# Upper weight words limited by one ScalarE step for all 16 tiles, and a new order of all engines, in a gated linear attention plus MoE kernel

## Chip, cores and metric

One core of a Trainium2 chip. The metric is the device time of one execution in microseconds (us), lower is better; before the change the median of three runs is 465.81 us (465.54 to 467.68).

## What is computed

```python
f = 1 / (1 + exp(-f_logit))                       # [4, 8, 768, 48]
state = 0                                         # [4, 8, 48, 48]
for t in range(768):
    state = f[:, :, t, :, None] * state + k[:, :, t] (outer) v[:, :, t]
    y[:, :, t] = q[:, :, t] @ state
x = y as [3072 tokens, 384]
h = x @ w_in                                      # 384 -> 2048
g = h * clip(h + 3, 0, 6) / 6
out = g @ w_out                                   # 2048 -> 384
```

All arrays are float32; the weights reach the kernel as float64 words (`w`, viewed as int64) and are turned on the chip into two fp32r parts, a high and a low one.

## The kernel before

The attention is cut into 24 units (4 batches times 6 chunks of 128 tokens). The MoE is cut into 6 groups of 512 tokens (the four units of one chunk) times 16 weight tiles `f`; step `n` of the MoE stands for group `n // 16` and tile `n % 16`. Everything is written out as one list of tokens, `ORDER`, from which the program emits the instructions; `after` chains each engine's instructions, so each engine runs its own instructions in exactly that order. `ON_POOL` names the tokens that GpSimd does in place of VectorE, `ON_ACT` those weight tiles whose limiting is done on ScalarE. A token is an operation and a number; a TensorE token also has the PSUM bank it writes.

Tokens of a unit, with the line of the kernel before: on SyncE's queue `load` L352 (gates), `loadq` L359 (q and k), `loadv` L364 and `hole` L568 (two copies into the gaps of the transposed activations `xts`); on ScalarE `gate` L369, `end` L395, `ktok` L470, `xh` L550, and `carry0`, `carry1` L495, L502 of units 0 to 3; on VectorE `back` L376, `rend` L392, `fwd` L400, `kmul` L389, `qmul` L405, `decay` L408 (the last three may be on GpSimd), `mask` L451, `xl` L563, `carry0`, `carry1` L497, L504 of the later units; on TensorE `tk` L463, `kv` L482, `att` L444, `qs` L514, `av` L531. In some units `xl` is done by TensorE and ScalarE (`ym` L554, `xl` L561).

Tokens of weight tile `f`: `ld` L256 (768 KB from HBM into `raw`), `z` L279 on ScalarE (rounds the word, into `w`), the limit of the upper 16 bits into `y`, `mid` L286, `dif` L291 and `top` L295 on VectorE (they put the exponent in place), `high` L307 on ScalarE, `low` L310 on VectorE (or in two parts `lowi`, `lowo`), `wd` L314 (a copy that keeps fp32 output weights). The limit is the subject: for the nine tiles of `ON_ACT` it is two ScalarE steps, `cy` L267 (relu of the word plus a bias, reading `raw` with a stride) and `lim` L271 (relu of a constant less that, in place); for the other seven it is one VectorE `lim` L273.

Tokens of a MoE step: `mm1` L599 (9 matmuls of 512 columns), `relu` L609 on ScalarE, `g` L613 on VectorE, `gh` L622 on ScalarE, `gl` L626 on VectorE or GpSimd, `mm2` L643 (9 matmuls). Tiles 0 to 2 of the first group are done in halves of 256 columns: `mm1a`, `mm1b` L665 (units 0 and 1, units 2 and 3), `relua` L674, `ga` L679, `mm2a`, `mm2b` L684. `warm` L822 and `tiny` L829 are matmuls on a blank tile with which TensorE fills time. Buffers are rings: `qkf` 3, `v` 3, `gates` 2, `tg` 3, `gg` 2, `w` 3, `y` 2.

Of the kernel before, what the change touches and what calls it, by code (L numbers as in the profile page):

```python
# [59 lines left out]
warm.2 carry0.1 mask.1 high.0 wd.0 qs.1.0 back.3 av.1 loadq.4 hole.0 att.2.2 xh.1 dif.1 kmul.3 warm.4 z.1 xl.1 load.4  # L60
mask.2 ktok.2 hole.1 lowi.0 cy.2 rend.3 top.1 tk.3.4 warm.2 ld.3 kv.2.2 ktok.3 lim.2 kv.3.0 fwd.3 carry0.2 z.2 warm.2
mid.2 qs.2.2 qmul.3 warm.2 carry1.3 dif.2 load.5 att.3.0 gate.4 ld.4 top.2 av.2 high.1 wd.1 mm1a.0.4 loadv.4 carry0.3
mask.3 lowi.1 end.3 carry1.2 loadq.5 xh.2 back.4 warm.1 high.2 ym.2 qs.3.0 relua.0 av.3 lowi.2 xl.2 kmul.4 lim.3
warm.1 xh.3 hole.2 mm1a.1.2 ga.0 end.4 xl.3 mm2a.0 relua.1 hole.3 decay.4 gate.5 ga.1 mid.3 z.3 rend.4 mm1a.2.1 dif.3
ld.5 fwd.4 wd.2 cy.4 ld.6 tk.4.4 mm2a.1 loadq.6 lim.4 qmul.4 top.3 ktok.4 ld.7 z.4 att.4.2 load.6 mid.4 ld.8 mm1b.0.4
back.5 relua.2 ld.9 high.3 ld.14 mm1b.1.0 ga.2 kmul.5 relub.0 rend.5 gb.0 cy.5 dif.4 kv.4.2 ld.10 mm1b.2.1 low.3 lim.5
loadv.5 top.4 mm2b.0 z.5 carry0.4 relub.1 mid.5 mm2a.2 mask.4 high.4 gb.1 cy.6 carry1.4 dif.5 mm2b.1 low.4 relub.2
lim.6 top.5 tk.5.0 mm1.3.3 z.6 mid.6 fwd.5 mm1.4.4 dif.6 qmul.5 relu.3 gb.2 end.5 high.5 g.3 decay.5 gate.6 low.5
att.5.2 ktok.5 mm2b.2 relu.4 back.6 top.6 qs.4.0 kmul.6 av.4 loadq.7 g.4 high.6 loadv.6 mask.5 loadv.7 mm1.5.4 gh.3
ld.12 lim.7 gh.4 load.7 low.6 ld.11 xh.4 gl.4 ld.15 gl.3 mm2.3 relu.5 rend.6 z.7 g.5 mid.7 z.8 lim.8 mm2.4 dif.7 gh.5  # L70
top.7 z.9 mid.8 mm1.6.2 high.7 dif.8 cy.9 low.7 end.6 top.8 kv.5.0 decay.6 relu.6 tk.6.4 lim.9 mm1.7.3 carry0.5 xl.4
gl.5 cy.10 mid.9 high.8 fwd.6 qs.5.0 relu.7 av.5 dif.9 qmul.6 mm2.5 xh.5 loadv.8 carry1.5 g.7 loadq.8 ktok.6 g.6 z.10
low.8 ym.5 lim.10 mm1.8.4 top.9 gate.7 gh.6 back.7 high.9 att.6.2 mid.10 gh.7 kv.6.0 kmul.7 gl.6 mm2.6 cy.11 rend.7
mask.6 lim.11 dif.10 z.11 low.9 tk.7.2 mm1.9.3 top.10 ktok.7 relu.8 fwd.7 high.10 end.7 relu.9 low.10 gl.7 mm2.7 g.8
carry0.6 gh.8 mm1.10.4 g.9 cy.12 carry1.6 qmul.7 xl.5 mid.11 load.9 gl.8 lim.12 mm2.8 ld.13 decay.7 hole.5 dif.11 gh.9
mid.12 z.12 dif.12 qs.6.2 top.11 att.7.0 loadq.9 top.12 av.6 high.11 load.8 kv.7.0 relu.10 gl.9 mm2.9 low.11 xh.6
carry0.7 mask.7 z.14 g.10 gate.9 qs.7.0 xl.6 z.13 lim.13 av.7 hole.6 mid.13 mm1.11.2 xh.7 lim.14 gh.10 loadv.9 dif.13
hole.4 mid.14 high.12 gl.10 mm2.10 top.13 relu.11 gate.8 g.11 low.12 gh.11 mm1.12.3 high.13 gl.11 carry1.7 xl.7 low.13
hole.7 mm1.13.4 dif.14 loadq.10 top.14 mm2.11 back.8 high.14 relu.12 low.14 kmul.8 z.15 mm1.14.1 lim.15 relu.13 g.12
g.13 mid.15 mm1.16.0 gh.13 dif.15 top.15 gl.13 tk.8.2 high.15 mm2.13 end.8 gh.12 low.15 relu.14 rend.8 gl.12 mm1.15.4  # L80
fwd.8 qmul.8 mm2.12 back.9 relu.15 load.10 relu.16 g.15 ktok.8 g.14 att.8.2 g.16 kv.8.2 gh.14 mm1.17.4 mask.8 gl.14
rend.9 gate.10 fwd.9 gh.15 mm2.14 gl.15 qmul.9 back.10 mm2.15 lowo.0 mm1.19.1 outs.0 outv.1 kmul.9 end.9 gh.16 outs.2
gl.16 decay.8 relu.17 mm1.18.0 od.2 rend.10 load.11 relu.19 g.17 od.0 carry0.8 fwd.10 mm2.16 relu.18 g.19 end.10
qmul.10 carry1.8 g.18 tk.9.3 kmul.10 load.12 lowo.1 mm1.20.4 loadv.10 ktok.9 od.1 gh.17 decay.9 gh.18 gl.17 gate.11
qs.8.0 back.11 att.9.2 decay.10 loadq.11 av.8 kv.9.2 gl.18 xh.8 mm2.17 gate.12 carry0.9 carry1.9 lowo.2 end.11 mask.9
mm1.21.2 gh.19 gl.19 xl.8 tk.10.3 relu.21 mm2.18 ktok.10 g.21 relu.20 rend.11 back.12 qs.9.0 gh.21 fwd.11 att.10.2
loadq.12 av.9 kv.10.0 qmul.11 mm2.19 g.20 load.13 loadv.11 carry0.10 gl.21 loadv.12 carry1.10 mm1.22.4 rend.12 fwd.12
kmul.12 mask.10 mm2.21 relu.22 g.22 decay.11 gh.22 kmul.11 mm1.23.3 gate.13 qmul.12 xh.9 back.13 load.14 hole.8
tk.11.4 relu.23 gl.22 mm2.22 ktok.11 xl.9 gh.20 g.23 hole.9 gl.20 qs.10.0 rend.13 att.11.2 gate.14 loadq.13 av.10
kv.11.0 loadv.13 tk.12.4 mm2.20 ktok.12 gh.23 end.12 gl.23 decay.12 mm1.24.4 mask.11 kmul.13 mm1.25.3 mm2.23 relu.25  # L90
relu.24 g.25 g.24 mm1.29.3 gh.24 gl.24 fwd.13 mm1.26.4 relu.29 gh.25 qmul.13 xh.10 gl.25 mm2.25 load.15 xl.10 relu.26
carry0.11 back.14 mm2.24 g.29 g.26 qs.11.0 gh.26 att.12.2 gl.26 av.11 kv.12.2 loadv.14 xh.11 carry1.11 mm2.26 mask.12
hole.10 gh.29 carry0.12 gate.15 carry1.12 loadq.14 rend.14 mm1.27.4 tk.13.2 relu.27 mm1.30.3 g.27 gl.29 xl.11 mm2.29
relu.30 hole.11 gh.27 g.30 end.13 kmul.14 mm1.28.1 gl.27 gh.30 ktok.13 gl.30 decay.13 back.15 tk.14.0 mm2.30 fwd.14
qmul.14 mm1.31.2 load.16 mm1.32.4 relu.31 relu.28 g.31 end.14 g.28 mm2.27 relu.32 ktok.14 qs.12.0 gh.28 att.13.2 gh.31
loadq.15 gl.28 av.12 kv.13.2 g.32 xh.12 mm2.28 decay.14 gate.16 mask.13 rend.15 carry0.13 carry1.13 fwd.15 mm1.33.4
xl.12 qmul.15 gl.31 qs.13.2 kmul.15 att.14.0 load.17 loadv.15 av.13 kv.14.0 xh.13 mm2.31 relu.33 xl.13 back.16 hole.13
tk.15.2 g.33 mm1.35.3 end.16 loadq.16 ktok.15 hole.12 carry0.14 gh.32 end.15 outs.3 outv.4 gl.32 decay.15 loadv.16
gate.17 mm1.36.2 rend.16 fwd.16 gh.33 outs.5 relu.35 mm2.32 g.35 qmul.16 carry1.14 gl.33 load.18 mm1.34.4 gh.35
kmul.16 back.17 mm2.33 relu.34 relu.36 g.34 g.36 tk.16.3 gl.35 gh.34 mm1.41.4 ktok.16 gl.34 mask.14 qs.14.2 att.15.0  # L100
loadq.17 decay.16 av.14 od.5 kv.15.0 xh.14 mm2.35 xl.14 mask.15 carry0.15 rend.17 mm2.34 fwd.17 gh.36 relu.41 qmul.17
g.41 qs.15.0 gl.36 gh.41 att.16.2 av.15 gl.41 kv.16.2 xh.15 mm2.36 gate.18 back.18 mm2.41 carry0.16 rend.18 xl.15
fwd.18 hole.15 mm1.38.4 carry1.16 loadv.17 mask.16 load.19 carry1.15 loadv.18 loadq.18 mm1.40.0 relu.38 mm1.37.3
relu.40 mm1.39.1 relu.37 g.37 qmul.18 g.38 mm1.44.3 kmul.17 gh.38 load.20 hole.14 g.40 gl.38 mm1.43.0 relu.39 gh.40
gl.40 mm2.38 g.39 relu.43 mm2.40 gh.37 end.18 gate.20 gl.37 g.43 mm1.42.1 kmul.18 gh.39 end.17 relu.44 gl.39 g.44
mm2.39 mm2.37 mm1.47.2 gh.44 gh.43 relu.42 gl.43 mm1.46.0 g.42 relu.47 gl.44 g.47 mm2.44 mm2.43 gh.42 gl.42 mm1.51.3
gh.47 relu.46 gl.47 back.20 mm1.45.2 g.46 tk.18.0 relu.45 mm2.42 ktok.18 g.45 relu.51 g.51 tk.17.4 gh.46 mm2.47
ktok.17 gl.46 gate.19 qs.16.0 gh.45 att.17.2 loadq.19 decay.18 gl.45 av.16 kv.17.0 mask.17 mm2.46 xh.16 decay.17
mm1.49.3 mm2.45 relu.49 g.49 carry0.17 xl.16 mm1.48.4 outs.6 back.19 outs.8 gh.51 od.8 od.3 qs.17.0 relu.48 att.18.2
# [857 lines left out]
```

## Time and profile before

| | |
|---|---|
| median of three runs | 465.81 us (465.54, 465.81, 467.68) |
| span of the profiled execution | 464.7 us (its own time is not listed apart) |
| TensorE busy | 453.4 us, 98% of the span |
| VectorE, ScalarE, GpSimd busy | 291.0, 212.4, 64.3 us |
| mean granted TensorE clock | 0.998 |
| chain that ended last | TensorE 90%, VectorE 3%, DMA 2%, ScalarE 2% |

Busy time of TensorE is an upper bound of its use, since matmuls are pipelined and their ends are modelled. The page divides the span in 40 slices of 11.6 us: VectorE is near full in the first 10 of them and at about half afterwards, ScalarE is busiest in the second to eighth, and the DMA engines are near full in the first five.

### The profile page before, as it was taken

How to read it: one execution, taken by the hardware profiler on the slowest of the kernel's cores; microseconds unless marked ns; L12 is line 12 of the kernel's file. 1: busy time of each engine (PE TensorE's matmuls, PEld its weight loads, DVE VectorE, ACT ScalarE, POOL GpSimd, SP SyncE). 2: the span in 40 equal slices, each digit the busy share in tenths (PEclk: the TensorE clock that was granted, in tenths of full speed). 3: DMA queues.
4: the chain of work that ended last, by engine and by line, in shares of the span. 5: the costliest groups of instructions: out<-in, count | busy, mean ns of one | idle time of the engine just before them, and what ended most of it. 6: DMA issues, size and time to landing. Idle time of an engine off the chain costs nothing.

```text
span 464.7 us, 11482 instructions
## 1 busy us (share of the span) xinstructions
PE 453.4 (98%) x4967; PEld 386.6 (83%) x4967; DVE 291.0 (63%) x455; ACT 212.4 (46%) x365; POOL 64.3 (14%) x65
## 2 busy tenths in 40 slices
...
GB/s 302 306 294 335 360 242 24 204 54 26 176 108 104 24 81 59 132 74 84 82 0 1 110 75 155 56 57 2 95 1 20 8 1 0 2 135 1 0 1 74
DMA packets 19113, 44.91 MB, mean 97 GB/s; under 512 B 2544, under 2 KB 8816, under 8 KB 19056
## 3 DMA queue, kind: packets, MB, share of 16 engines
...
q14 instruction: 16, 0.13, 0.1%
...
## 4 chain that ended last, share of the span: by engine, by line
PE 90%; DVE 3%; DMA 2%; ACT 2%; issue 1%; SPq 0%; POOL 0%; POOLq 0%
PE o L643 35%; PE pair L599 26%; PE single L599 11%; PE pair L514 3%; PE pair L444 2%; DMA v<-unit 2%; PE pair L531 2%; PE o L684 2%; PE idle L822 2%; PE pair L482 2%; PE pair L699 1%; PE single L699 1%; PE pair L463 1%; PE pair L665 1%; ACT w L279 1%
## 5 line engine op out<-in xcount | busy, mean ns | idle before, releaser
L643 PE MATMUL o<-gg,weight 128*128 128x512 f32 x705 | 165.7, 382 | 0.4 <-DVE gg L626 0.3
L643 PEld LDWEIGHTS o<-gg,weight 128*128 128x128 f32 x705 | 131.1, 189 | 19.8 <-DVE gg L626 1.6
L599 PE MATMUL pair<-xts,weight 128*128 128x512 f32 x576 | 133.1, 381 | 0.0
L599 PEld LDWEIGHTS pair<-xts,weight 128*128 128x128 f32 x576 | 107.6, 189 | 15.1 <-DVE tg L613 0.3
L626 DVE TENSOR_TENSOR gg<-tg,gg 128x512 fp32r<-128x512 f32 x75 | 56.0, 751 | 55.6 <-ACT gg L622 55.4
L622 ACT ACTIVATE gg<-tg 128x512 fp32r<-128x512 f32 x79 | 48.9, 626 | 65.7 <-PE o L643 51.3
L613 DVE SCALAR_TENSOR_TENSOR tg<-tg,pair 128x512 f32<-128x512 f32 x64 | 43.4, 683 | 55.8 <-ACT tg L609 55.6
L609 ACT ACTIVATE tg<-pair,half 128x512 f32<-128x512 f32 x64 | 43.5, 684 | 72.4 <-PE pair L599 69.1
L599 PE MATMUL single<-xts,weight 128*128 128x512 f32 x261 | 61.9, 382 | 0.0
L599 PEld LDWEIGHTS single<-xts,weight 128*128 128x128 f32 x261 | 48.5, 189 | 7.0 <-DVE tg L613 0.2
L609 ACT ACTIVATE tg<-single,half 128x512 f32<-128x512 f32 x29 | 19.9, 685 | 32.8 <-PE single L599 29.2
L376 DVE TENSOR_TENSOR_SCAN suffix<-gates,unit 112x516 f32<-112x516 f32 (+1 forms) x25 | 29.4, 1180 | 4.2 <-ACT gates L369 4.2
L400 DVE TENSOR_TENSOR_SCAN gates<-gates,rend 112x516 f32<-112x516 f32 x24 | 30.4, 1266 | 0.3
L389 POOL TENSOR_TENSOR qkf<-qkf,suffix 112x512 f32<-112x512 f32 x14 | 21.1, 1507 | 64.7 <-DVE suffix L376 22.2
L613 DVE SCALAR_TENSOR_TENSOR tg<-tg,single 128x512 f32<-128x512 f32 x29 | 19.8, 682 | 9.9 <-ACT tg L609 9.6
L408 POOL TENSOR_TENSOR decayed<-state,ends 112x192 f32<-112x192 f32 x13 | 10.6, 819 | 109.8 <-PE pair L514 65.8
L405 POOL TENSOR_TENSOR qkf<-qkf,gates 112x512 f32<-112x512 f32 x11 | 15.8, 1437 | 67.0 <-DVE gates L400 39.3
L550 ACT ACTIVATE xts<-pair 112x512 fp32r<-112x512 f32 x24 | 14.2, 594 | 23.6 <-PE pair L531 19.0
L451 DVE TENSOR_TENSOR a<-pair,causal 128x512 f32<-128x512 f32 x24 | 16.4, 683 | 8.2 <-PE pair L482 5.3
L643 PE MATMUL o<-xts,weight 128*128 128x512 f32 x84 | 20.3, 380 | 0.0
L563 DVE TENSOR_TENSOR xts<-pair,xts 112x512 fp32r<-112x512 f32 x21 | 14.4, 684 | 7.6 <-ACT xts L550 7.6
L626 DVE TENSOR_TENSOR xts<-tg,xts 128x512 fp32r<-128x512 f32 x14 | 9.5, 690 | 13.9 <-ACT xts L622 13.9
...
## 6 DMA issues: line engine op xcount, KB each, us to landing
...
```

The lines of the kernel that those rows point to most:

```text
L376: nc.vector.tensor_tensor_scan(flat(sf[:, p])[:, ::-1], gt[:, columns(p)][:, ::-1], flat(unit[:, p])[:, ::-1], 0.0, op0=ALU.mult, op1=ALU.add,
L389: engine("kmul", i).tensor_tensor(parts_of(t, 1), parts_of(t, 1), split(sf[:, :, 1:C + 1]), op=ALU.mult)
L400: nc.vector.tensor_tensor_scan(past, past, flat(rend), 0.0, op0=ALU.mult, op1=ALU.add)
L405: engine("qmul", i).tensor_tensor(parts_of(t, 0), parts_of(t, 0), split(to), op=ALU.mult)
L451: nc.vector.tensor_tensor(d["a"].rearrange("r p e t -> r e p t"), d["at"], causal.unsqueeze(1).unsqueeze(1).broadcast_to([128, 2, NP, HC]) ...
L563: nc.vector.tensor_tensor(parts(1), d["y"][:PR], parts(0).bitcast(F32), op=ALU.subtract)
L599: nc.tensor.matmul(h, win(f, a, k), turned(g["xt"][:, k, :g["n"] // C, b]), start=i == 0, stop=i == 3 * KT - 1,)
L609: nc.scalar.activation(d["t"], d["h"], AF.Relu, bias=half, scale=1.0 / 6.0)
L613: nc.vector.scalar_tensor_tensor(d["t"], d["t"], 1.0, d["h"], op0=ALU.min, op1=ALU.mult)
L622: nc.scalar.activation(d["gg"][:, 0], d["t"], AF.Copy)
L626: engine("gl", g["first"] + f).tensor_tensor(d["gg"][:, 1], d["t"], d["gg"][:, 0].bitcast(F32), op=ALU.subtract)
L643: nc.tensor.matmul(g["o"][m], wout(f, a, m), halves_of(g[f]["gg"][:, b]), start=f == 0 and i == 0, stop=f == NF - 1 and i == 2, skip_group ...
```

## The change

The two ScalarE steps of a limit become one: relu of `TOP_LAST` less the word, read with the stride from `raw`, no lower limit first. All 16 tiles take it (before: nine in two ScalarE steps, seven in one VectorE step). `mid`'s bounds follow (they are shifted by `TOP_LAST` in place of `SPAN - LOWEST`). `ON_POOL` and `ORDER` are new tables. Tokens by engine, before and after: ScalarE 9 `cy` and 9 `lim`, after 16 `lim`; VectorE 7 `lim`, after none; `gl` 89 on VectorE and 4 on GpSimd, after 65 and 28; `warm` 40 matmuls, after 31; `ym` 3 units, after 2. All other tokens stay in number, up to a few of `kmul`, `qmul`, `decay`, `lowo`, `outs` that change engines.

```diff
 ON_ACT = """
-lim.1 lim.2 lim.4 lim.5 lim.6 lim.9 lim.10 lim.11 lim.12
+lim.0 lim.1 lim.2 lim.3 lim.4 lim.5 lim.6 lim.7 lim.8 lim.9 lim.10 lim.13 lim.12 lim.11 lim.14 lim.15
 """.split()
 ORDER = """
-load.0 warm.13 tiny.12 loadq.0 load.1 loadv.0 loadv.1 loadq.1 ld.0 gate.0 back.0 rend.0 kmul.0 gate.1 fwd.0 tk.0.0
...
+load.0 load.1 loadv.0 loadq.0 ld.0 loadv.2 loadq.1 gate.0 loadv.1 gate.1 back.0 rend.0 fwd.0 end.0 kmul.0 qmul.0
...
-    LOWEST, SPAN = 32768 - TOP_ONE, 32768 - TOP_ONE + TOP_LAST
...
-    def conv_top(f):
-        nc.scalar.activation(joint(f, "y", U16), upper_of(f), AF.Relu, bias=lowest)
-
     def conv_limit(f):
         if on_scalar(f):
-            nc.scalar.activation(conv[f]["y"], conv[f]["y"], AF.Relu, bias=span, scale=-1.0)
+            nc.scalar.activation(joint(f, "y", U16), upper_of(f), AF.Relu, bias=topmost, scale=-1.0)
         else:
...
         if on_scalar(f):
-            low, high = SPAN - LOWEST - TOP_ONE, SPAN - LOWEST + TOP_ONE
+            low, high = TOP_LAST - TOP_ONE, TOP_LAST + TOP_ONE
```

Line numbers after the change are up to 6 lower.

TensorE, about where the first MoE matmuls stand. Before (`qkf_272` is unit 3, `weight_359`, `weight_548`, `weight_573` are tiles 0, 1, 2; L444 is `att.3`, L531 `av`, L554 `ym.2`, L514 `qs.3`):

```order
L444 MATMUL pair_73<-qkf_272 64x64 x16
L531 MATMUL pair_74<-a_419,v_300 64x64 x8
L531 MATMUL pair_74<-a_419,v_300 48x64 x8
L665 MATMUL single<-xts,weight_359 128x256 x9
...
L554 MATMUL pair_74<-xts,minus 112x256 x2
L514 MATMUL pair_73<-qkf_272,middle_106 64x64 x8
...
L665 MATMUL pair_74<-xts,weight_548 128x256 x9
L684 MATMUL o_0_625<-th_0_585,weight_359 128x256
```

After (`qkf_273` is unit 3, `weight_319`, `weight_543`, `weight_553` are tiles 0, 1, 2):

```order
L438 MATMUL pair_73<-qkf_273 64x64 x16
L659 MATMUL single<-xts,weight_319 128x256 x9
L659 MATMUL pair_73<-xts,weight_543 128x256 x9
L508 MATMUL pair_74<-qkf_273,middle_104 64x64 x8
L525 MATMUL pair_74<-a_548,v_280 64x64 x8
L525 MATMUL pair_74<-a_548,v_280 48x64 x8
L659 MATMUL pair_73<-xts,weight_553 128x256 x9
L678 MATMUL o_0_618<-th_0_569,weight_319 128x256
```

The first two halves of MoE work now stand ahead of `qs.3` and `av.3`, no `ym` and no fill lies between, and all three `mm1a` stand ahead of the first `mm2a`.

ScalarE, about the conversion of tiles 1 and 2. Before (`raw_220` and `raw_304` are tiles 1 and 2; L550 is `xh`, L307 `high`):

```order
L550 ACTIVATE xts<-pair_73 112x2x2x128
L279 ACTIVATE w_415<-raw_220 128x768
L470 ACTIVATE ktok_421<-single 128x448
L267 ACTIVATE y_426<-raw_304,lowest 128x768
L470 ACTIVATE ktok_462<-single 128x448
L271 ACTIVATE y_426<-y_426,span 128x768
```

After (`raw_260` and `raw_275` are tiles 1 and 2; L265 is the one limit, L544 `xh`, L555 `xl`):

```order
L464 ACTIVATE ktok_364<-single 128x448
L265 ACTIVATE y_368<-raw_260,topmost 128x768
L544 ACTIVATE xts<-pair_74 112x2x2x128
L555 ACTIVATE xts<-pair_74 112x2x2x128
L496 ACTIVATE state_110<-pair_73 112x2x2x48
L273 ACTIVATE w_422<-raw_260 128x768
```

The limit of tile 1 now stands right ahead of `xh.1`, so `xh.1` waits for that tile's load; before, tile 1 had been limited right ahead of `gate.3`, and `xh.1` waited for no load.

SyncE's queue, at the start. Before (`v_152`, `qkf_149` are unit 0, `v_154`, `qkf_156` unit 1, `raw_158`, `raw_220` tiles 0 and 1):

```order
L352 DMA gates_76<-unit 128x259
L359 DMA qkf_149<-unit 128x1024
L352 DMA gates_78<-unit 128x517
L364 DMA v_152<-unit 128x400
L364 DMA v_154<-unit 128x400
L359 DMA qkf_156<-unit 128x1024
L256 DMA raw_158<-w 128x3072
L352 DMA gates_76<-unit 128x517
L256 DMA raw_220<-w 128x3072
```

After (`v_123`, `qkf_125` are unit 0, `qkf_131`, `v_135` unit 1, `v_129` unit 2, `raw_127` and `raw_260` tiles 0 and 1):

```order
L346 DMA gates_76<-unit 128x259
L346 DMA gates_78<-unit 128x517
L358 DMA v_123<-unit 128x400
L353 DMA qkf_125<-unit 128x1024
L255 DMA raw_127<-w 128x3072
L358 DMA v_129<-unit 128x400
L353 DMA qkf_131<-unit 128x1024
L358 DMA v_135<-unit 128x400
L346 DMA gates_76<-unit 128x517
L353 DMA qkf_194<-unit 128x1024
L346 DMA gates_78<-unit 128x517
L255 DMA raw_260<-w 128x3072
```

Unit 0's q and k are now the fourth load instead of the second, tile 0 stands ahead of unit 1's q and k, and tile 1 stands behind the gates of units 2 and 3, of which the second waits for `qmul.1`.

## Rows read from the trace of the kernel before

**Rows 1.** Busy time of each engine in two stretches, with their columns.
```profile
core 0: us, PE busy (x) PEld busy (x) DVE busy (x) ACT busy (x) POOL busy (x), PEclk, DMA share, GB/s
...
42.00:96.00 54.00, 53.32 (x658) 43.94 (x658) 52.83 (x85) 44.96 (x66) 16.94 (x11) 1.00 0.59 214
96.00:460.00 364.00, 363.90 (x3594) 317.43 (x3592) 202.42 (x316) 137.55 (x244) 37.59 (x30) 1.00 0.18 56
```
**Rows 2.** Timeline of TensorE, 28 to 37 us: start, duration, instructions, [idle before].
```profile
28.61 1.27 PE L665 MATMUL single<-xts,weight 128*128 128x256 f32 x9
...
30.28 0.46 PE L514 MATMUL pair<-qkf,middle 48*64 48x64 f32 x16
...
35.70 0.55 PE L463 MATMUL single<-ident,qkf 112*128 112x112 f32 x4
36.09 1.47 PE L684 MATMUL o<-th,weight 128*128 128x256 f32 x6
```
**Rows 3.** Timeline of VectorE in the first 32 us, same columns.
```profile
13.52 1.23 DVE L376 TENSOR_TENSOR_SCAN suffix<-gates,unit 112x516 f32<-112x516 f32 x1 [0.82 <-ACT gates L369]
...
14.88 0.53 DVE L291 TENSOR_TENSOR y<-y,t 128x768 int16<-128x768 int16 x1
15.33 1.22 DVE L400 TENSOR_TENSOR_SCAN gates<-gates,rend 112x516 f32<-112x516 f32 x1
16.47 1.02 DVE L295 SCALAR_TENSOR_TENSOR w<-y,w 128x768 int16<-128x768 int16 x1
17.45 0.36 DVE L286 TENSOR_SCALAR t<-y 128x768 uint16<-128x768 uint16 x1
...
28.81 0.69 DVE L451 TENSOR_TENSOR a<-pair,causal 128x512 f32<-128x512 f32 x1 [0.94 <-PE pair L531]
...
31.00 1.60 DVE L273 TENSOR_SCALAR y<-raw 128x768 int16<-128x768 int16 x1
```
**Rows 4.** Timeline of ScalarE, 26 to 30 us.
```profile
26.56 0.63 ACT L369 ACTIVATE gates<-gates 112x512 f32<-112x512 f32 x1 [0.34 <-DMA gates<-unit]
...
28.26 0.33 ACT L495 ACTIVATE middle<-pair 112x192 f32<-112x192 f32 x1 [0.33 <-PE pair L444]
...
29.44 0.85 ACT L307 ACTIVATE weight<-w 128x768 fp32r<-128x768 f32 x1
```
**Rows 5.** Groups of instructions by line: busy us, mean ns of one.
```profile
L267 ACT ACTIVATE y<-raw,lowest 128x768 uint16<-128x768 int16 x9 | 10.1, 1121 | 0.0
L271 ACT ACTIVATE y<-y,span 128x768 uint16<-128x768 uint16 x9 | 8.4, 930 | 0.2
L273 DVE TENSOR_SCALAR y<-raw 128x768 int16<-128x768 int16 x7 | 6.5, 933 | 0.0
L609 ACT ACTIVATE tg<-pair,half 128x512 f32<-128x512 f32 x64 | 43.5, 684 | 72.4 <-PE pair L599 69.1 <-DVE gg L626 3.2
L613 DVE SCALAR_TENSOR_TENSOR tg<-tg,pair 128x512 f32<-128x512 f32 x64 | 43.4, 683 | 55.8 <-ACT tg L609 55.6
L622 ACT ACTIVATE gg<-tg 128x512 fp32r<-128x512 f32 x79 | 48.9, 626 | 65.7 <-PE o L643 51.3 <-DVE tg L613 14.3
L626 DVE TENSOR_TENSOR gg<-tg,gg 128x512 fp32r<-128x512 f32 x75 | 56.0, 751 | 55.6 <-ACT gg L622 55.4
```
**Rows 6.** Tile gg on GpSimd: ns min/median/max of the four `gl`.
```profile
L626 POOL TENSOR_TENSOR gg<-tg,gg x4: 1282/1285/2522, 55.4 to 110.7; 128x512 fp32r<-128x512 f32 x4
```
**Rows 7.** Timeline of GpSimd at 31 us.
```profile
30.87 1.27 POOL L389 TENSOR_TENSOR qkf<-qkf,suffix 112x512 f32<-112x512 f32 x1 [1.86 <-PE pair L514]
```
**Rows 8.** Landing of unit 0's q and k, issued at 1.27 us.
```profile
DMA to landing us min/median/max: 3.8/3.8/3.8
```
**Rows 9.** Landing of weight tile 1, issued at 8.32 us.
```profile
DMA to landing us min/median/max: 6.3/6.3/6.3
```
**Rows 10.** Landing of unit 4's gates, issued at 21.93 us.
```profile
DMA to landing us min/median/max: 4.6/4.6/4.6
```
**Rows 11.** Landing of three `hole` copies, issued between 32.3 and 34.7 us.
```profile
DMA to landing us min/median/max: 2.4/2.8/4.3
```

More of the change, by code (lines that the diff above doesn't have):

```diff
@@ L60 @@
[L60 to L109, printed above, removed]
@@ new lines @@
+warm.13 tiny.12 tk.0.2 back.1 load.2 ktok.0 att.0.0 loadq.2 kv.0.3 rend.1 mask.0 carry0.0 fwd.1 carry1.0 lim.0 warm.2
+qs.0.2 av.0 qmul.1 z.0 kmul.1 load.3 ld.1 mid.0 warm.4 tk.1.1 dif.0 loadq.3 ld.2 top.0 ktok.1 loadv.3 gate.2 warm.3
+kv.1.0 back.2 carry1.1 carry0.1 kmul.2 end.2 xh.0 rend.2 fwd.2 end.1 high.0 warm.6 ym.0 tk.2.4 xl.0 att.1.0 wd.0
+gate.3 hole.0 mask.1 qs.1.2 ktok.2 lowi.0 qmul.2 lim.1 av.1 back.3 kv.2.0 xh.1 rend.3 ym.1 fwd.3 xl.1 carry1.2 kmul.3
+hole.1 z.1 warm.3 att.2.2 mask.2 tk.3.4 carry0.2 load.4 ktok.3 ld.3 qs.2.2 qmul.3 mid.1 av.2 loadq.4 dif.1 lim.2 top.1
```

126 lines of the change are left out of this document (85 added, 41 removed).

## Prediction

> **What bounds the kernel now.** I first cut the span into stretches. From 96 us to 460 us TensorE is busy 363.90 us of 364, while VectorE has 202.42 and ScalarE 137.55 [rows 1]: there the program is a row of matmuls without a gap, and no work taken from another engine can shorten it. From 42 to 96 us TensorE is busy 53.32 of 54, so 0.7 us are open, with VectorE at 52.83 and ScalarE at 44.96: all three are near full, and relief shows only if TensorE asks for weights sooner. What is left is the head. TensorE starts its first MoE matmul at 28.61, reaches qs.3, the last unit of the first group, at 30.28, and at 35.70 it has done the attention of four units, three mm1a and one mm2a [rows 2]. In those 28 us it waits for others and runs fills; VectorE carries the chain (scans, limits, exponent steps), and reaches mask.3 at 28.81 [rows 3]. So the time after is the time before, less what the head gets shorter, plus what new waits cost behind it.
>
> **Part 1, the work removed.** The new ScalarE limit has the strided 16-bit read of cy and the scale and bias of lim. Its price lies between lim's 0.93 us and cy's 1.12 [rows 5]; I take 1.12, since the read is cy's. ScalarE: 9 x (1.12 + 0.93) = 18.5 us go, 16 x 1.12 = 17.9 come: -0.6 us in all, -3.6 at the low bound. VectorE: 7 x 0.93 = 6.5 us go. Besides, 24 gl of 0.75 us go from VectorE to GpSimd [rows 5], 18 us, nearly all behind 96 us, where VectorE had 160 us free. So the step itself saves ScalarE little; it frees VectorE of two limits in the first 32 us and of five more up to 100.
>
> The Trainium skill gives a price too (ScalarE: Activation LUTs, What ACT_TABLE_LOAD costs): about 280 ns plus 0.833 ns per column for a step with a pointer bias, an estimate of 0.92 us for 768 columns. The row of lim agrees with it, that of cy, which reads with a stride, is 0.2 us above; by the page ScalarE would save 3.8 us in all, and my sum does not change, since ScalarE has 9 us open in 42 to 96.
>
> **Part 2, the head, walked along the new order.** Unit 0's q and k are now issued fourth, at about 2.2 us, and landed 3.8 us after their issue before [rows 8]: 6.0 if that holds, 7.2 if the 0.45 MB put ahead of them cost 1.2 us more. fwd.0, moved ahead of kmul.0, fills VectorE to 6.6 anyway. I take 6.6 for kmul.0. From there to mask.3 VectorE has, from one start to the next [rows 3]: three back with rend (13.52 to 14.88, 1.36 each) 4.1; three fwd (15.33 to 16.47, 1.14) 3.4; three times mid, dif and top (0.28 + 0.45 + 0.98) 5.1; ten kmul, qmul and mask (0.69 less the 0.09 by which neighbours overlap) 6.0. Sum 18.6 us, so 25.2 without a wait. Two waits I find by following the other engines with the same rows. att.1 stands behind ym.0, that behind xh.0, that on ScalarE behind end.2, which needs back.2 and so load.2, still issued after qmul.0: att.1 ends 0.7 us after VectorE is ready for mask.1. And ld.1, now behind load.3, is issued near 12.4 and lands 6.3 us later as before [rows 9], at 18.7; lim.1 waits for it, xh.1, ym.1 and xl.1 follow at 21.5, att.2 behind them, which costs mask.2 another 0.6. So mask.3 at 26.5, against 28.81.
>
> Next TensorE. hole.1 is issued after xl.1, two copies of 0.6 us, and load.4 now stands behind it: 22.8, landing 4.6 us later [rows 10], 27.4. gate.4 (0.63), high.2 (0.85) and carry0.3 (0.33) follow on ScalarE [rows 4]: qs.3 at 29.1. Until then mm1a.0 and mm1a.1 are done, which before came mostly later. av.3 and mm1a.2 end at 31.1, three mm2a at 1.4 us each (1.47 less overlap, [rows 2]) at 35.2. Before, the same work was done at 35.70 + 2 x 1.4 = 38.5. Lead 3.3 us.
>
> mm1b.0 then waits for hole.3. xl.3 ends at 32.2, the second copy is issued at 32.9 and lands 2.8 us later [rows 11], 35.7; tk.4 covers up to 35.5. Cost 0.2 (1.7 at that row's 4.3). Lead 3.0.
>
> **Part 3, from there to 96 us.** The cover here is ScalarE and VectorE. With 0.7 us open on TensorE before, at most 0.7 can be won. To hold the lead both engines must deliver 3 us sooner in 54: VectorE loses five limits (4.7 us), ScalarE had 9 us free and keeps its load (six times 0.93 go, five times 1.12 come). I take +0.2.
>
> **Part 4, behind 96 us.** Nothing can be won; a new order can only open gaps. I looked at each step for what stands on TensorE between mm1 and mm2. The tightest is step 36: mm2.34 and mm1.44, 2 x 1.94 = 3.9 us, for relu, g, gh (0.68 + 0.68 + 0.63) and a gl on GpSimd (1.28 to 2.52, [rows 6]): 3.3 to 4.5, a wait of 0 to 0.7. All other steps have 5.5 or more. Units 12 to 18 now come in one run, and by the same kind of walk unit 18's q, k and v have 1 to 2 us to spare after their buffers come free. I take -0.5; bounds 0 and -3.
>
> **The sum.** 3.0 + 0.2 - 0.5 = 2.7 us. The profiled span is 464.7, 1.1 below the runs' median, which holds what lies around it; the difference goes on the median: 465.8 - 2.7 = 463.1. A change under 0.5% (2.3 us) can't be told from none here.
>
> **Rivals.** (A) The forecast: a lead of 1.5 to 4.5 us kept, 461.3 to 464.3, chance 0.60.
>
> (B) The lead is there but is spent: the walk has some twenty handovers, and each load it rests on came up to 2.5 us later than others of its kind. If q and k land at 7.2, hole.3 at 4.3 and the attention run loses 0.5 us more, 0.6 + 1.5 + 0.5 go: 465.7. For it: the page shows the DMA engines near full in the first five slices. Against: VectorE's own sum (25.2) leaves 3.6 us under 28.81. Chance 0.25, 464.3 to 466.5.
>
> (C) More than forecast: the two waits of VectorE don't come and mid-kernel losses vanish: +1.3 + 0.5, and none of the -0.5: 460.8. Chance 0.08.
>
> (D) Slower: GpSimd becomes what mm2 waits for. A subtract there takes 1.28 us alone and 2.52 at worst [rows 6] against 0.75 on VectorE [rows 5], and two engines slow each other: a VectorE limit took 1.60 us instead of 0.93 beside a GpSimd multiply at 30.87 [rows 3, 5, 7]. If each of the 24 moved gl came 1.8 us late and a third of TensorE's steps had no slack, 8 x 1.8 = 14 us would be lost; it decides against the lead from about two such steps (2.7 / 1.8), and ends slower by 0.5% from three. Against it: only one step has under 4 us of cover. Five waits of 1.8 give 463.1 + 9.0 = 472.1; chance 0.07, 467 to 473.
>
> The Trainium skill has the rule behind (D) (SBUF — State Buffer, Who interferes with whom): GpSimd and a VectorE instruction with two SBUF inputs share a port pair as an exclusive lock, so one waits for the whole of the other. By it the 24 gl would hold VectorE up by as much as 24 x 1.28 = 31 us, within the 160 it has free there; the trace shows such stretched steps, and TensorE without a gap beside them.
>
> That the limit costs as before (say 2 us in one step) would add ScalarE 14 us before 96 us and undo the lead; cy, with the same read, has a mean of 1.12 [rows 5], so it is left to (D)'s share.
>
> **How the numbers follow.** Likeliest 463.1, (A)'s own range 461.3 to 464.3. With (B) above and (C) below, 460.8 to 465.8 leaves (D), and some of (B), out. Faster by over 0.5% means under 463.5: (C), and four fifths of (A) (0.48), 0.56; within 0.5%: the rest of (A) and (B), 0.36; slower 0.08.
>
> **What the profile after should show.** The new limit at 1.05 to 1.2 us, 16 of them; qs.3 near 29 and three mm2a done near 35; mm1b.0 behind a hole copy by under 1 us; TensorE again without a gap from 42 us on. It is wrong if kmul.0 waits for its load beyond 7.5, if lim.1 or gate.4 wait for DMA longer than stated, or if TensorE waits for gl on GpSimd or for unit 16 to 18's loads by more than a microsecond in sum.

## The result, and the profile after

The changed kernel takes 472.15 us (median of four runs, 470.80 to 473.05) against 465.77 (465.54 to 467.68): ratio 1.0122, 95% interval 1.0097 to 1.0147. The forecast was 463.1. In its profiled execution, which is the longest of the four, the span is 470.9 us, 6.2 above before.

Busy time in the two stretches of [rows 1]:

```profile
core 0: us, PE busy (x) PEld busy (x) DVE busy (x) ACT busy (x) POOL busy (x), PEclk, DMA share, GB/s
42.00:96.00 54.00, 52.74 (x723) 44.91 (x722) 52.74 (x86) 46.52 (x66) 14.43 (x11) 1.00 0.58 221
96.00:460.00 364.00, 360.47 (x3549) 312.99 (x3548) 186.63 (x287) 137.77 (x244) 65.17 (x52) 1.00 0.19 56
```

Behind 96 us TensorE is idle for 3.5 us, where it was idle for 0.1. That is only half of the loss: it is also busy for longer on the same work, since dependent pieces follow each other directly. To see both I measured each piece of TensorE's work (an `mm1`, an `att`, a `qs` ...) from its start to the start of the next, and took off the usual pitch of such a piece (the lower quartile over both kernels). Behind 96 us this excess adds up to 5.9 us before and 12.5 after, 6.6 us more. Where the first 96 us end, the two have done the same work (all of units 0 to 7, `mm1` to 13, `mm2` to 10) at 96.08 and 95.73 us: of the 3.2 us of lead that the forecast had there, 0.35 came. So in this profile the change lost its 6.2 us behind 96 us, and its head won next to nothing.

The groups of the limit and of `gl`, for [rows 5, 6]:

```profile
L265 ACT ACTIVATE y<-raw,topmost 128x768 uint16<-128x768 int16 x16 | 18.1, 1129 | 2.2 <-DMA raw<-w 2.2
L620 POOL TENSOR_TENSOR gg<-tg,gg 128x512 fp32r<-128x512 f32 x28 | 40.6, 1451 | 135.1 <-ACT gg L616 103.6 <-ACT ends L389 16.2 <-DVE state L498 12.0
L620 DVE TENSOR_TENSOR gg<-tg,gg 128x512 fp32r<-128x512 f32 x51 | 38.1, 752 | 41.0 <-ACT gg L616 41.0
```

**Handovers.** The clearest new thing is in the attention of the later units. TensorE's timeline at unit 8, first after, then before (L508 or L514 is `qs`, L525 or L531 `av`, L438 or L444 `att`):

```profile
131.11 0.69 PE L438 MATMUL pair<-qkf 48*64 48x64 f32 x32
131.63 0.40 PE L508 MATMUL pair<-qkf,decayed 48*48 48x64 f32 x16
131.85 0.40 PE L508 MATMUL pair<-qkf,middle 48*48 48x64 f32 x16
132.34 0.66 PE L525 MATMUL pair<-a,v 64*48 64x64 f32 x32
```
```profile
123.78 0.44 PE L514 MATMUL pair<-qkf,decayed 48*48 48x64 f32 x16
124.04 0.40 PE L514 MATMUL pair<-qkf,middle 48*48 48x64 f32 x16
124.27 0.65 PE L444 MATMUL pair<-qkf 48*64 48x64 f32 x32
124.73 0.63 PE L531 MATMUL pair<-a,v 64*48 64x64 f32 x32
```

`av` adds to the PSUM tile that `qs` has begun, and the program makes it wait for the last `qs`:

```python
hold = nc.tensor.nop()
after(hold.ins, d["qs"], mybir.DependencyClass.Sync)
```

Before, the next unit's `att` lies between, and from the start of `qs` to the start of what follows it 0.48 us pass. After, `av` follows at once, and it is 0.71. In units 8 to 19, twelve times, the new order has it so (0.71 to 0.84 us); before it stood so behind 96 us only in unit 23. That is 3.3 us of the 6.6, and the idle column shows little of it. Only the program's own form was run, in which a wait for the last `qs` stands ahead of `av`: how much of the price is the wait and how much the shared tile is not shown. Single waits are the next part: on VectorE's carry, on a load of v, and one on "issue" (that is, put down to nothing that the profile shows):

```profile
156.58 0.60 PE L457 MATMUL pair<-ident,qkf 112*128 112x112 f32 x4 [0.84 <-DVE state L498]
244.95 0.57 PE L476 MATMUL pair<-v,ktok 64*48 64x48 f32 x32 [0.77 <-DMA v<-unit]
266.15 2.10 PE L593 MATMUL single<-xts,weight 128*128 128x512 f32 x9 [0.60 <-issue]
```

**The head.** VectorE at `kmul.0`, at `mid`, `dif` and `top` of tile 1 (L280, L285, L289) and at `mask.3`, TensorE from `tk.0` on, and SyncE's queue at the second pair of `hole` copies and `load.4`, for [rows 2, 3]:

```profile
7.75 0.69 DVE L383 TENSOR_TENSOR qkf<-qkf,suffix 112x512 f32<-112x512 f32 x1 [1.15 <-DMA qkf<-unit]
...
25.23 0.40 DVE L280 TENSOR_SCALAR t<-y 128x768 uint16<-128x768 uint16 x1
25.66 0.56 DVE L285 TENSOR_TENSOR y<-t,y 128x768 int16<-128x768 uint16 x1
26.32 1.05 DVE L289 SCALAR_TENSOR_TENSOR w<-y,w 128x768 int16<-128x768 int16 x1
27.27 0.33 DVE L280 TENSOR_SCALAR t<-y 128x768 uint16<-128x768 uint16 x1
...
29.22 0.70 DVE L445 TENSOR_TENSOR a<-pair,causal 128x512 f32<-128x512 f32 x1
```
```profile
8.54 0.57 PE L457 MATMUL pair<-ident,qkf 112*128 112x112 f32 x4 [1.97 <-DVE qkf L383]
9.10 1.13 PE L438 MATMUL pair<-qkf 48*64 48x64 f32 x32
10.00 1.46 PE L476 MATMUL pair<-v,ktok 64*64 64x48 f32 x48
...
30.06 1.24 PE L659 MATMUL pair<-xts,weight 128*128 128x256 f32 x9 [0.87 <-DVE a L445]
31.23 0.46 PE L508 MATMUL pair<-qkf,middle 48*64 48x64 f32 x16
...
37.39 0.55 PE L457 MATMUL single<-ident,qkf 112*128 112x112 f32 x4
39.12 2.25 PE L659 MATMUL pair<-xts,weight 128*128 128x256 f32 x18 [1.19 <-DMA xts<-xts]
```
```profile
19.52 6.49 SPq L562 DMA_DIRECT2D xts<-xts  x4
26.10 0.53 SPq L346 DMA_DIRECT2D gates<-unit  x1
```

TensorE waited 1.97 us for the late q and k, and then ran at half its clock: an `att` takes 1.13 us where it takes 0.69 elsewhere.

```profile
core 0: us, PE busy (x) PEld busy (x) DVE busy (x) ACT busy (x) POOL busy (x), PEclk, DMA share, GB/s
6.00:9.05 3.05, 1.08 (x18) 0.75 (x16) 1.90 (x4) 0.00 (x0) 0.00 (x0) 1.00 0.98 372
9.05:12.47 3.42, 3.42 (x87) 2.45 (x90) 3.35 (x5) 1.47 (x4) 0.00 (x0) 0.50 1.00 362
```

### The profile page after: what moved, and what is told of

Same layout as the page of the kernel before. It is cut to its first block, busy times and chain, and to the rows that moved or that the text cites. A ratio compares the mean times of both kernels' runs of the same rounds, so it can differ in the third digit from the quotient of the medians.

```text
span 470.9 us, 11458 instructions
## 1 busy us (share of the span) xinstructions
PE 454.6 (97%) x4956; PEld 389.1 (83%) x4956; DVE 275.8 (59%) x429; ACT 213.4 (45%) x363; POOL 87.5 (19%) x83
## 4 chain that ended last, share of the span: by engine, by line
PE 87%; DMA 6%; DVE 4%; issue 1%; ACT 1%; SPq 1%; DVEq 0%; ACTq 0%
PE o L637 34%; PE pair L593 28%; PE single L593 9%; DMA qkf<-unit 3%; PE pair L525 3%; PE pair L508 3%; PE pair L438 2%; PE pair L476 2%; PE pair L693 1%; PE single L693 1%; DMA gates<-unit 1%; PE single L457 1%; DVE suffix L370 1%; DMA v<-unit 1%; PE pair L457 1%
## 5 line engine op out<-in xcount | busy, mean ns | idle before, releaser
L593 PE MATMUL pair<-xts,weight 128*128 128x512 f32 x612 | 140.9, 380 | 0.0
L593 PEld LDWEIGHTS pair<-xts,weight 128*128 128x128 f32 x612 | 114.8, 189 | 16.8 <-DVE tg L607 0.8
L620 POOL TENSOR_TENSOR gg<-tg,gg 128x512 fp32r<-128x512 f32 x28 | 40.6, 1451 | 135.1 <-ACT gg L616 103.6
L620 DVE TENSOR_TENSOR gg<-tg,gg 128x512 fp32r<-128x512 f32 x51 | 38.1, 752 | 41.0 <-ACT gg L616 41.0
L593 PE MATMUL single<-xts,weight 128*128 128x512 f32 x225 | 53.5, 383 | 0.6 <-issue 0.6
L593 PEld LDWEIGHTS single<-xts,weight 128*128 128x128 f32 x225 | 42.0, 189 | 6.7 <-issue 0.5
L603 ACT ACTIVATE tg<-single,half 128x512 f32<-128x512 f32 x25 | 17.1, 683 | 19.3 <-PE single L593 16.5
L544 ACT ACTIVATE xts<-pair 112x512 fp32r<-112x512 f32 x24 | 14.2, 591 | 21.4 <-PE pair L525 13.1
L383 POOL TENSOR_TENSOR qkf<-qkf,suffix 112x512 f32<-112x512 f32 x12 | 15.7, 1311 | 30.4 <-DMA qkf<-unit 10.3
L607 DVE SCALAR_TENSOR_TENSOR tg<-tg,single 128x512 f32<-128x512 f32 x25 | 17.0, 681 | 4.9 <-ACT tg L603 4.7
L265 ACT ACTIVATE y<-raw,topmost 128x768 uint16<-128x768 int16 x16 | 18.1, 1129 | 2.2 <-DMA raw<-w 2.2
```

The costliest lines, as they stand in the source:

```text
L265: nc.scalar.activation(joint(f, "y", U16), upper_of(f), AF.Relu, bias=topmost, scale=-1.0)
L383: engine("kmul", i).tensor_tensor(parts_of(t, 1), parts_of(t, 1), split(sf[:, :, 1:C + 1]), op=ALU.mult)
L593: nc.tensor.matmul(h, win(f, a, k), turned(g["xt"][:, k, :g["n"] // C, b]), start=i == 0, stop=i == 3 * KT - 1,)
L603: nc.scalar.activation(d["t"], d["h"], AF.Relu, bias=half, scale=1.0 / 6.0)
L607: nc.vector.scalar_tensor_tensor(d["t"], d["t"], 1.0, d["h"], op0=ALU.min, op1=ALU.mult)
L620: engine("gl", g["first"] + f).tensor_tensor(d["gg"][:, 1], d["t"], d["gg"][:, 0].bitcast(F32), op=ALU.subtract)
```

## The experiments

Diffs of the order show the tokens of the engine concerned alone, without what stands between them for other engines. Theory H: handovers and other small losses of TensorE's new order behind 96 us. Theory L: late loads at the start, and the clock behind them. Theory C came up with the first runs: TensorE's own code comes late. Rivals: D of the prediction (GpSimd's `gl`), and S, that the one-step limit itself costs. The kernel before was run again beside every experiment; its median there was 465.6 to 466.2, and the ratios are to it. Each experiment left one trace, which need not be of its median run.

**e1, att (once a tk) back between qs and av**, at 13 places like this one.

```diff
-qs.9.3 av.9 att.10.0 kv.10.0
+qs.9.3 att.10.0 av.9 kv.10.0
```


> The changed kernel with only TensorE's order touched: in 13 units the next unit's att (once a tk) is put between qs and av, as the order before had it. Theory H (handovers on TensorE): av waits for the last write of qs where nothing lies between, 0.72 to 0.84 us from qs to av in place of 0.48, 3.6 us in all; so 468.5 us (467.9 to 469.2), and qs to its follower at 0.48 in the trace. Rival D (mm2 waits for gl on GpSimd) and rival L (all of the loss is late loads): 472.1, no change.

474.91 us (470.68 to 475.13): nothing won. In the profile `qs` to its follower is mostly 0.48 us, and 3.0 of the 3.3 us are gone from there. But the wait ahead of `tk.11` has grown from 0.84 to 1.53 us, the clock falls behind it (some 1.7 us, half of the stretch), `tk.15` now waits 0.5 us for GpSimd's `kmul`, and the excess behind 96 us is still 12.4. So taking the handovers out of the new order does not by itself give their time back:

```profile
158.88 0.60 PE L457 MATMUL pair<-ident,qkf 112*128 112x112 f32 x4 [1.53 <-DVE state L498]
```
```profile
160.66:164.07 3.41, 3.41 (x80) 3.01 (x72) 2.59 (x5) 1.11 (x2) 1.29 (x2) 0.50 0.02 5
```

**e2, the one step in the old order**, the other seven tiles on VectorE as before.

```diff
-cy.1 lim.1
+lim.1
```


> The order and the engine tables of before, with one edit: the nine tiles limited on ScalarE take the one step in place of two. Theory H (the loss is the new order's, not the new step's): ScalarE loses nine steps of 0.93 us, six of them ahead of 96 us; TensorE's rows are those of before, so 464.8 us (463.8 to 465.8). Rival S (the single step is slower in place or holds its neighbours up, and that is what was lost): 468 or more.

467.67 us (465.15 to 470.42), ratio 1.0045 (1.0020 to 1.0069). Its profile, one of its lowest runs, has a span of 463.4 us and `qs.3` at 29.33 us, 1 us sooner than before. Both expectations are missed: the step alone shows 1.7 us of the 6.4 in the medians (0.9 to 3.2 by the interval), so S is out as the cause of all of it, but theory H's gain is not there either. In this one profile two stops of TensorE that the profile before had at 27 and 33 us (0.31 and 0.46 us) are missing, so its lower span is not all the step's.

**e3, gl back on VectorE.**

```diff
 ON_POOL
-gl.9 low.12 gl.11 gl.12
+low.12 gl.11
```


> The changed kernel with 26 gl put back from GpSimd to VectorE at the same places of the order. Theory H: VectorE has the time, TensorE waited for no gl, so 472.1 (471.4 to 472.8). Rival D: the waits of mm2 for gl on GpSimd go, 469 or less.

475.13 us (473.32 to 476.38), no lower than e1 and e4, which ran beside it, and 2.3 us above the range that theory H gave (its profile has a stop of 4.1 us in the head, as e4's). TensorE's waits of the changed kernel name no `gl`; D is out.

**e4, q and k early.**

```diff
-load.0 load.1 loadv.0 loadq.0 ld.0
+load.0 loadq.0 load.1 loadv.0 ld.0
```


> The changed kernel with unit 0's q and k issued second, as before, in place of fourth. Theory H: kmul.0 near 6.4 us in place of 7.75, tk.0 near 7.0 in place of 8.54, TensorE's wait of 2 us ahead of it under 0.6 and no stretch of 1.2 GHz behind it, so the head is 1.0 to 2.0 us shorter; what is left of that at the end 0.5 to 1.5: 471.1. Rival: the head is set by later loads (units 2 to 4, tiles 1 and 5), 472.1.

473.74 us (470.57 to 475.27). `tk.0` starts at 7.50 us in place of 8.54 and `kv.2` at 19.92 in place of 21.11, as L says; there is no fall of the clock at 9 us (nor in the second profile of the changed kernel, e5 below, where TensorE waited 2.80 us ahead of `tk.0` and `kv.2` starts at 20.38). And then TensorE stops for 4.1 us inside `kv.2`, waiting for nothing that the profile knows.

**What that stop is.** The same stop is in every profile with the new head and its code in place, always 36 matmuls into `kv.2`: 0.46 us in the first profile of the changed kernel, 4.37 when it ran again (e5). First after, then e5, and e5's clock behind it:

```profile
21.11 0.73 PE L476 MATMUL pair<-v,ktok 64*64 64x48 f32 x36
22.30 0.38 PE L476 MATMUL pair<-v,ktok 64*64 64x48 f32 x12 [0.46 <-issue]
```
```profile
20.38 0.73 PE L476 MATMUL pair<-v,ktok 64*64 64x48 f32 x36
25.48 0.56 PE L476 MATMUL pair<-v,ktok 64*64 64x48 f32 x12 [4.37 <-issue]
```
```profile
24.70:34.94 10.24, 9.34 (x185) 7.28 (x185) 5.13 (x9) 6.41 (x11) 1.57 (x1) 0.50 0.54 185
```

The page of the changed kernel lists a DMA queue that carries instructions:

```profile
q8 instruction: 41, 0.67, 0.6%
```

That is 41 packets of 16 KB, each about 1 us long. I numbered TensorE's records (weight loads, matmuls, semaphores) in order of time. The stops of the head fall at records 705, 961 and 1217, that is 256 apart, and each ends 1.1 to 1.6 us after a packet of q8 has ended. For the block that begins at record 705 (us; "asked" is the time at which record 449, the block end before it, was passed):

```
kernel                    asked   packet starts     ends    record 705   gap before it
before                    16.43   19.80 (+3.37)    20.82      23.08          0.29
after                     17.00   19.91 (+2.91)    20.87      22.30          0.67
e5_after_again            16.15   23.08 (+6.93)    24.16      25.48          4.59
e1_av_spaced              15.92   21.38 (+5.46)    22.53      23.60          2.94
e4_q0_first               14.97   22.27 (+7.30)    23.28      24.75          4.31
e8_ld2_later              15.52   18.77 (+3.25)    19.73      21.19          0.93
e9_head_loads             14.88   20.71 (+5.83)    21.68      22.98          2.67
e13_loads_timed           14.92   19.26 (+4.34)    20.24      21.51          1.85
```

Theory C: a block is asked for when the end of the one before last is passed, its packet waits among the loads, and TensorE, which runs 256 records of small matmuls off in as little as 2.4 us (units 16 and 17 of the kernel before), comes to the end first. In all profiles the packets of the first 45 us started 0.4 to 10.2 us behind that point. Where the DMA engines were over 90% busy in the 2 us behind it, the packet came 1.0 to 10.2 us later, half of them over 3.2; where they were under 5% busy, at most 2.6. Behind 45 us many packets started up to 4.5 us ahead of it, so these records do not show what asks for a block; that the loads hold the packet up is an argument from this, no run shows it alone. The Trainium skill (Runtime: NRT & Kernel Launch, Instruction fetch mechanics) has the blocks of 256 instructions and 16 KiB, and calls the cost of crossing from one to the next mostly hidden. The first agrees with these rows, the second does not hold in this head.

**e11, the block ends moved.**

```diff
-warm.13 tiny.12
+warm.1 tiny.80
```


> The changed kernel with the 13 warm and 12 tiny matmuls at the start turned into 1 warm and 80 tiny ones, about as long, so that every later TensorE instruction stands 112 places further on in the code. Theory C (it stops where a block of 256 instructions ends): no stop 36 matmuls into kv.2; if it stops, then 56 matmuls earlier, 12 into av.1. Rival (a wait for data of kv.2: v or ktok): the stop stays at the same matmul of kv.2. The time is no test, 470 to 476, since the small fills may leave another clock.

`kv.2` runs through, and no stop comes earlier in the head; in units 16 and 17 TensorE now stops inside `kv`, at records 256 apart, where it did not before. Time 475.64 us (474.54 to 476.96), no test as said.

```profile
21.27 0.87 PE L476 MATMUL pair<-v,ktok 64*64 64x48 f32 x48
...
253.91 0.40 PE L476 MATMUL pair<-v,ktok 64*48 64x48 f32 x16 [1.24 <-issue]
...
261.98 0.30 PE L476 MATMUL pair<-v,ktok 64*48 64x48 f32 x8 [1.54 <-issue]
```

**e5, the changed kernel again, and e8, tile 2's load behind the hole copies.**

```diff
-ld.1 loadq.3 ld.2 loadv.3 wd.0 hole.0 hole.1
+ld.1 loadq.3 loadv.3 wd.0 hole.0 ld.2 hole.1
```


> The changed kernel once more, unaltered, as the one that the others of this call are held against. Theory C (late code): in the head TensorE runs its instructions off faster than the next block of 256 comes, which waits on a DMA engine behind the loads; it stops at the same instruction, 36 matmuls into kv.2, in every execution, for 0.5 to 4.5 us, and the time goes with the length of that stop: 471 to 476 us. Rival L (late data): the stops move about with the loads.

> The changed kernel with the load of weight tile 2 (768 KB) moved on SyncE's queue from ahead of unit 3's v to behind the first hole copies, some 5 us later. Theory C: the block of code asked for at about 15 to 17 us has 2 us less ahead of it on its DMA engine, so the stop inside kv.2 falls to 0 to 2 us and no stretch of 1.2 GHz follows it: 2 to 4 us under the changed kernel of this call. Rival L: the load was not in the way and lim.2 now waits for it: the same or 1 to 2 us slower.

e5 472.56 us (470.89 to 476.44), e8 473.14 (471.88 to 473.56). In e8 the packet starts 3.25 us after it is asked for, where e5 has 6.93, the stop is 0.72 us by the profile, and the clock stays at 2.4 GHz. But the first profile of the unaltered kernel has 2.91 and 0.46, so e8 does not show that the moved load did it. And `lim.2` now waits for its load. So e11 shows that the stop belongs to the end of a code block, and no run has won its price back:

```profile
26.93 1.06 ACT L265 ACTIVATE y<-raw,topmost 128x768 uint16<-128x768 int16 x1 [2.34 <-DMA raw<-w]
```

**e6 and e7, one half of each order**, spliced near 96 us.

> The new order up to mm2.13 near 96 us, where both orders have done the same work, then the order and GpSimd's share of before. Theory H (the part behind 96 us loses 6.2 to 6.6 us by qs, av and other attention work put without anything between, by code that comes late for the run of units 12 to 18, and by some waits): 6 us below the changed kernel of this call, so 466 to 469. Rival (the whole loss is the head's): as the changed kernel.

> The order and steps of before up to mm1.13 near 96 us, then the new order and GpSimd's share. Theory H: 6.0 to 6.6 us above before, 471.5 to 473, and with less spread than the changed kernel, whose head varies. Rival (the loss is the head's): 465 to 467.

e6 468.33 us (465.76 to 470.77), 4.2 under e5; its splice itself costs 1.9 us (`mm2.11` and `mm1.14` wait). e7 477.74 (475.93 to 478.71), 11.9 over before, of which by an estimate from its profile some 4 are the splice's: a wait of 2.2 us for `gh` at 96 us and 3.41 us of 1.2 GHz behind it. Both say that the new part behind 96 us is what costs. e7 leaves some 8 us for it, more than the 6.2; its profile has one more stop for code there (0.5 us) and a wait for GpSimd (0.4).

**e9, e13, e10, e14, other places for two loads**: q and k second in all; tile 2's load behind `wd.0` (e9), or ahead of the hole copies once `xl.0` is done (e13); e10 and e14 are the same heads with the old order behind 96 us.

```diff
-load.0 load.1 loadv.0 loadq.0 ... ld.2 loadv.3 wd.0 hole.0
+load.0 loadq.0 load.1 loadv.0 ... loadv.3 wd.0 ld.2~xl.0 hole.0
```


> The changed kernel with two loads moved on SyncE's queue: unit 0's q and k second in place of fourth, weight tile 2 behind the copy wd.0 (about 1.7 us later) in place of ahead of unit 3's v. Theory C (code that comes late behind the loads): tk.0 near 7.5 us, the block asked for at about 15 us starts within 4 us, TensorE's stop inside kv.2 is under 1.5 us, no stretch of 1.2 GHz between 8 and 40 us; so 469 to 471 us. Rival: the two loads only change places with others that are then late, 472 to 474.

> The changed kernel with unit 0's q and k issued second, and weight tile 2 issued ahead of the first hole copies but only when xl.0 is done, near 18 us: behind the time at which the block of code is asked for (15 us), ahead of the time at which lim.2 wants it (25 us). Theory C: the block starts within 3.5 us, the stop inside kv.2 is under 1 us, TensorE stays at 2.4 GHz from 8 to 40 us, mask.3 does not wait for lim.2 as it did with the load at 20 us; the head is 2 to 3 us shorter than in the changed kernel as measured first, 468 to 470 us. Rival (code, clock and loads only trade places): 472 and more.

> The head of e9_head_loads up to mm2.13, then the order and GpSimd's share of before, with mm2.11 put behind mm1.16 so that it does not wait for its gl. Theory H with C (6.2 us lost behind 96 us by the new order, the rest in the head by loads and code): 463 to 465.5, at or under before. Rival (the new head has no lead to keep): 466.5 to 469.

> The head of e13_loads_timed up to mm2.13, then the order and GpSimd's share of before (gl.11 on VectorE). Theory C with H: e13 less 4.5 to 6, so 463 to 465, under before. Rival: 466 to 468, as the version with the loads less well placed.

e9 471.96 us (470.46 to 474.05), e13 472.01 (470.33 to 473.71), e10 468.43 (466.88 to 470.28), e14 466.50 (464.86 to 468.08). In the profiles the stop in `kv.2` is 2.5, 1.6, 2.7 and 2.7 us: I did not get the packet out from behind the loads. The pair e13, e14 differs behind 96 us alone: 5.5 us in the medians, and 12.25 against 6.77 = 5.5 in the excess. (In e10 the splice itself costs some 3.5 us: `mm1.16` waits 1.9 us for a weight, and the clock falls behind it.) In all four the expectation of theory C is missed and the times are the rival's or next to it. e14 is 1.2% faster than the changed kernel and equal to before (ratio 1.0004, 0.9983 to 1.0025); no version here beats before.

**e12, handovers outside the dense run.** In it step 29's `g` reads the transposed k of unit 11 in place of its h, as `tk.11` writes that bank first.

```diff
-tk.11.0 qs.10.2 ktok.11 av.10 att.11.0
+tk.11.4 qs.10.2 ktok.11 att.11.0 av.10
```


> e9_head_loads with TensorE's order touched behind 42 us, outside the run of units 12 to 18: in seven units att or tk stands between qs and av (0.24 to 0.27 us each, 1.85 in all), and tk.11 writes another bank, so that it does not wait for carry1.10 (0.8 to 1.0 us). Theory H: 2.4 to 2.8 us under e9_head_loads. Rival (what is won at one place is waited for at the next): within 0.7 us of it.

474.71 us (472.84 to 475.20), 2.7 over e9. `tk.11` waits 1.6 us again, now for a `relu`, and the clock falls for 3.41 us at 160.7, as in e1. So what is won at one place is lost at the next, as the rival said, and more; it tells nothing of the handover's price.

**e15, the old order with one step and the block ends moved by 40.**

```diff
-warm.13 tiny.12
+warm.11 tiny.34
```


> The old order with one ScalarE step in place of two, as in e2_old_order_one_step, and 40 places more of code ahead of the attention (11 warm and 34 tiny matmuls for 13 and 12), so that by its trace no block of 256 is run off in under 4.7 us in the head (before 4.1). Theory C: the stops of 0.5 to 0.8 us at 27 and 33 us go, and 464.5 to 466 in place of 467.7. Rival (its spread comes from elsewhere): 467 to 468.

467.16 us (466.31 to 470.60), ratio 1.0035 (1.0010 to 1.0059). The gaps at its block ends at 28 and 33 us are 0.01 and 0.43 us (0.53 and 0.73 before), and `kv` waits up to 1.7 us for `ktok`; the time is the rival's.

**e16 and e17, one suspect each put into the kernel before.** e16, at 15 places:

```diff
-qs.8.0 att.9.2 av.8 kv.9.2
+qs.8.0 av.8 att.9.2 kv.9.2
```


> The kernel before, its order touched at 15 places alone: in units 8 to 22 av is put right behind qs, ahead of the next unit's att, as the changed kernel has most of them. Theory H (av waits for the last write of qs, 0.27 us where nothing lies between): 15 x 0.27 = 4.0 us above before, 469.2 to 470.4. Rival (TensorE catches it up elsewhere, since it is not always what others wait for): under 1 us above before.

472.05 us (470.19 to 472.19), ratio 1.0115 (1.0096 to 1.0135). In the profile `qs` to `av` costs 4.1 us more and the span is 4.0 longer (468.7). The medians differ by 5.9, of which the profile leaves 1.9 without a place. So in the old order the handover's price is real and nothing hides it.

```profile
123.39 0.44 PE L514 MATMUL pair<-qkf,decayed 48*48 48x64 f32 x16
123.65 0.40 PE L514 MATMUL pair<-qkf,middle 48*48 48x64 f32 x16
124.14 0.66 PE L531 MATMUL pair<-a,v 64*48 64x64 f32 x32
124.63 0.65 PE L444 MATMUL pair<-qkf 48*64 48x64 f32 x32
```

```diff
-load.0 loadq.0 load.1 loadv.0 loadv.1 loadq.1 ld.0
+load.0 load.1 loadv.0 loadq.0 ld.0 loadv.1 loadq.1
```


> The kernel before with its first loads in about the order of the changed kernel: unit 0's q and k fourth in place of second, weight tile 0 ahead of unit 1's. Theory L (late first load, and the clock behind the wait): kmul.0 near 6.5 to 7.5 us in place of 5.35, TensorE waits 1 to 2 us ahead of tk.0, with a stretch at 1.2 GHz behind it; 0.5 to 2 us above before, 466.5 to 468. Rival (later loads of the head set its end): within 0.5 us of before.

468.21 us (467.79 to 471.47), ratio 1.0045 (1.0030 to 1.0059). In its profile, which is of its longest run, `kmul.0` starts at 7.55 us after waiting 2.10 for its load, TensorE waits 1.28, and its clock falls (the mean clock of its six runs is 0.988 to 0.992, that of the kernel before beside them 0.992 to 1.000):

```profile
10.04:20.28 10.24, 9.53 (x168) 5.99 (x161) 9.61 (x16) 5.55 (x10) 1.18 (x1) 0.50 0.85 285
```

## Why the prediction was wrong, step by step

- **Part 1** held: 1129 ns, 16 times; forecast 1.12 us.
- **Part 2, first step, failed.** `kmul.0` at 7.75 us, not 6.6: q and k came 5.5 us after an issue at 2.21, not 3.8. The sum had called this covered by `fwd.0`, and priced nothing behind it, though it named 7.5 us as a sign of being wrong. By e17 the new order of the first loads costs the old kernel 2.1 us, the lower clock behind TensorE's wait included.
- **The rest of Part 2** was 2 to 3 us early: `mask.3` 29.22 (26.5). Of these 2.7 us 1.15 are `kmul.0`'s; VectorE's waits up to there came to 1.3 us, as forecast but at other places, and its steps to 20.1 (18.6). The three runs of `mid`, `dif` and `top` took 6.1 (5.1): the sum had priced `dif` at 0.45 us, the time to a step that does not need it, and `top`, which does, starts 0.66 behind it. Then `load.4` issued 26.10 (22.8), since its queue stood behind `hole.1`, which waited for `xl.1`; `qs.3` 31.23 (29.1), behind `mm1a.1`, which had stood 0.87 us for `mask.3`, since it writes the bank that `mask.3` reads (no term); three `mm2a` done 37.39 (35.2), `mm1b.0` waiting 1.19 for `hole.3` (0.2). Lead at 96 us 0.35 us (3.2). That is the spent lead of rival B.
- **What Part 2 had no term for**: TensorE stops where a block of its code ends. The old order ran the same pieces with fills and waits between, so the block mostly came in time; the new order packs `att`, `qs`, `av` and `kv` of two units into 5 us. In this one profile it cost 0.5 us; in others up to 4.4, with a longer stretch of 1.2 GHz behind it.
- **Part 3** held in size: the excess of TensorE's pieces from 42 to 96 us is 4.2 us, 4.4 before.
- **Part 4 failed, and this decides the sign.** I looked at what covers the chain from `mm1` to `mm2` and at loads, and took -0.5; it measured -6.2 to -6.6 in profiles, -5.5 between e13 and e14. That chain was covered, as forecast. What I did not look at was TensorE's own rows, in the order in which it runs them: twelve `av` right behind `qs` (3.3 us; e16 shows that price in the old order), `tk.11` behind a carry (0.8), `kv.15` behind a load (0.8), a stop for code right behind unit 18's `att` (0.6), and further handovers of 0.1 to 0.2 us each at `att` and `tk`. That the new part behind 96 us costs 5.5 us or more is shown by e6, e7 and the pair e13, e14; how it divides is read from the rows, and e1 and e12, which took handovers out again, won nothing.
- **Rival D** gave the right number, 472.1, by luck: no `mm2` waits for GpSimd, and e3 is no faster.

Open: why the one step alone in the old order (e2, e15) is 0.4% slower over all runs, though e2's profile was 1.3 us shorter than that of before; only one run of each has a trace. And how the head's loss of the changed kernel divides between loads, code and clock in a median run, since these trade places: e4, e8, e9 and e13 each took one away, and none was faster.
